# A fused retention and mixture-of-experts kernel: another head, and another order of all instructions

## The chip, the cores and the metric

The kernel runs on one core of a Trainium2 chip. The metric is the time of one execution on the device, in microseconds (us). Engines go by short names: PE is the matrix engine, DVE the vector engine, ACT the scalar engine, POOL is GpSimd and SP the engine that issues most of the transfers. Each engine runs its own instructions in order, and engines wait for each other by semaphores.

## The reference

A linear attention with decay (8 heads of 64, 768 tokens, 4 sequences) gives `x`, and a causal softmax attention of four experts with a gate that picks two of them gives the output. Cut to what matters:

```python
gamma = 1.0 - 2.0 ** (-5.0 - np.arange(H))            # one decay for each head
for t in range(S):
    state = gamma[None, :, None, None] * state + np.einsum('bhd,bhe->bhde', k[:, :, t], v[:, :, t])
    y[:, :, t] = scale * np.einsum('bhd,bhde->bhe', q[:, :, t], state)
x = y.transpose(0, 2, 1, 3).reshape(B, S, H * D)      # 4 x 768 x 512
logits = x @ w_gate                                   # top 2 of 4 experts, softmax over the two
for e in range(E):
    q, k, v = x @ wq[e], x @ wk[e], x @ wv[e]         # 64 columns each
    a = softmax(causal(scale * q @ k.T))
    out += (weight of e for the token) * (a @ v @ wo[e])
```

Everything is fp32. Products that need it are made of three: an operand is split into a high part (`_hi`, `oh`, `xh`) and the rest (`_lo`, `ol`, `xl`), and high times high, high times low and low times high are summed.

## The kernel before, in words

The loop over tokens is done in chunks. Within a chunk, q·k products are masked by `causal` and multiplied into v; what earlier chunks left is a state of 64x64 for each head, multiplied with q; the decays are put in as factors of the position, on k and v before and on the result after. The first sequence begins with three chunks of 128 tokens (`wide`, chunks 0 to 2), because nothing else is there yet to keep PE busy; later chunks have 64 tokens.

`head` (from line 1145) records this beginning. In it stand the loads (`load`, `const`, `wload`); a memset of `wu` on POOL and eight products of `wu` with itself (line 1199), whose results nobody reads; for each wide chunk the q·k products (line 438) into two PSUM tiles, two evictions by DVE that multiply with the mask (line 445), the scaling of v, and from chunk 1 on of k, by the decays in `kd3` (line 426: DVE in chunk 0, POOL in chunks 1 and 2), the masked products with v (line 465), the products of k and v that build the state in PSUM (line 478) and its eviction `sblk` (line 485), and from chunk 1 on the products with the state (line 496). Lines 511 to 515 scale the result by the decays `yb`, which one product with two rows spreads over all partitions (line 1203; ScalarE copies it, line 1205), and split it into `xh` and `xl`. The weights are split in `wsplit` (line 216 on ScalarE, line 217 on DVE or POOL) into `vg_hi` and `vg_lo`, `qk_hi` and `qk_lo`. The gate and value products (line 605, 36 products) follow, then the first projections to q and k (line 563).

After the head, three streams are merged for each following part of a sequence: the chunks of 64 tokens (lines 332, 336, 346 for the state, 391, 397, 405 for the chunk itself), the projections, and the softmax attention (line 739 scores, 790 mask, 809 and 832 to 850 row maxima, 756 exponentials, 875 and 897 sums, 931 products with v, 1033 to 1045 norm and split, 1064 output product). Evictions of the output (lines 1074 and 1078) go into three buffers `ot` and from there to memory (line 1081).

The order is not that of the code. Every operation is recorded by `op` with its engine, what it reads and writes, and a cost; a written table `ORDER` of operation numbers then says in which order all are issued, and `SLOTS` which buffer of its pool each tile takes. Within an engine the order in `ORDER` is the order of execution; a transfer into a buffer waits for the last reader of what stood in it, and with it wait all transfers behind it on SP.

Of the kernel before, what the change touches and what calls it, by code (L numbers as in the profile page):

```python
# [11 lines left out]
AF = mybir.ActivationFunctionType  # L12
# [7 lines left out]
NWARM = 8  # L20
# [89 lines left out]
def tile_retention_moe_attention(  # L110
# [74 lines left out]
    def const(src, shape, name):  # L185
# [5 lines left out]
        op("SP", 0.4, lambda: nc.sync.dma_start(t, src), w=[(name,)], nbytes=n)  # L191
        return t
# [47 lines left out]
    def load(g, which=(0, 1)):  # L240
# [172 lines left out]
    WR = {}  # L413
# [4 lines left out]
    def wide_v(g):  # L418
        nb = LD[g, 1]
        scale = ((1, 0, "v"),) if not g else ((1, 0, "v"), (0, g, "k"))  # L420
        for which, n, tok in scale:
            eng, cost, e = ("DVE", dve_c(512), nc.vector) if not g else ("POOL", pool_c(512), nc.gpsimd)

            def fn(e=e, which=which, n=n):
                x = nb.t[:, which].rearrange("p (h d) -> p h d", d=D)
                e.tensor_tensor(x, x, K["kd3"][:, n, :, None].to_broadcast([128, H, D]), op=OP.mult)  # L426

            op(eng, cost, fn, r=[(nb, tok), ("cst_t",)], w=[(nb, tok)])

    def wide_r1(g):  # L430
# [4 lines left out]
        def fn():  # L435
            for s in range(HP):
                for rt in range(2):
                    nc.tensor.matmul(ps[rt].t[:, s * C:(s + 1) * C], qb.t[rows(rt), 1, s], qb.t[rows(rt), 0, s],
                                     start=True, stop=True)

        op("PE", 512 * 4 * COL + 0.05, fn, r=[(qb, "q"), (qb, "k")], w=[(b,) for b in ps] + [(b, "n") for b in am],
           new=[*ps, *am], mode="64x128")
        for rt in range(2):
            def ev(rt=rt):
                nc.vector.tensor_tensor(am[rt].t.rearrange("p u h t -> p (u h t)").rearrange("p (s t) -> p s t", s=HP),
                                        ps[rt].t.rearrange("p (s t) -> p s t", s=HP),
                                        causal[:, None].to_broadcast([128, HP, C]), op=OP.mult)
# [1016 lines left out]
```

## Time and profile before

The median of 3 runs is 295.76 us (295.52 to 295.77).

| what | before |
|---|---|
| profiled execution | 296.57 us, of which the span is 294.90 |
| PE busy | 286.5 us, 97% of the span |
| DVE busy | 233.3 us, 79% |
| POOL busy | 152.1 us, 52% |
| ScalarE busy | 119.5 us, 41% |
| chain that ended last | PE 89%, DVE 5%, DMA 4% |
| first product, first projection, last product | 1.86, 25.69, 289.94 us |

The profiled execution is one run; the span runs from the first to the last instruction that the profiler saw, and 1.67 us lie around it. An engine's busy time counts overlapped matmuls as pipelined; the chain follows back, from the last instruction, what released each step.

### The profile page before, as it was taken

The page shows a single profiled execution, that of the slowest core. Times are in us where ns is not written, and L with a number is a line of the kernel's source. Part 1 is how long each engine was busy: PE and PEld are TensorE (multiplying, and loading weights), DVE is VectorE, ACT ScalarE, POOL GpSimd, SP SyncE. Part 2 cuts the span into 40 slices and gives each one's busy share as a digit, 9 for nine tenths or more (in the row PEclk, how much of TensorE's full clock was granted, in tenths as well). Part 3 has the DMA queues.
Part 4 walks back from the last instruction along what each step waited for, and adds up shares of the span by engine and source line. Part 5 has one row for each costly group of instructions (what it writes and reads, how often), then busy time and mean ns, then how long its engine had stood idle before and what let it go on. Part 6 is the DMA issues. An engine that isn't in the chain of part 4 may idle for free.

```text
span 294.9 us, 10349 instructions
## 1 busy us (share of the span) xinstructions
PE 286.5 (97%) x4283; PEld 250.8 (85%) x4283; DVE 233.3 (79%) x571; ACT 119.5 (41%) x273; POOL 152.1 (52%) x199
## 2 busy tenths in 40 slices
PE   7899999999999999999999999999999999999993
PEld 3699999988979799898898799998889988977773
DVE  1596478999999688899978468998988888988850
ACT  2151423335433352434542443345533435365462
POOL 2669541343149986235896368305835733089300
PEclk9999999999999999999999999999999999999998
DMA  7995585986874577328915765446204633264023
GB/s 236 408 364 209 181 215 178 250 234 163 253 235 153 153 218 230 101 77 219 320 54 156 247 185 173 96 137 184 57 1 131 179 104 104 53 185 150 15 107 110
DMA packets 22275, 50.33 MB, mean 171 GB/s; under 512 B 4178, under 2 KB 8786, under 8 KB 22228
## 3 DMA queue, kind: packets, MB, share of 16 engines
q1 hardware_dynamic: 22084, 49.60, 55.0%
q8 instruction: 34, 0.56, 0.8%
q14 instruction: 13, 0.11, 0.1%
q10 hardware_dynamic: 144, 0.07, 0.1%
HBM read 30.47 MB, written 6.60 MB: 126 GB/s over the span
## 4 chain that ended last, share of the span: by engine, by line
PE 89%; DVE 5%; DMA 4%; SPq 1%; POOL 1%; issue 0%; ACT 0%; DVEq 0%; POOLq 0%
PE ps L563 22%; PE ps L739 16%; PE ps L931 12%; PE ps L605 12%; PE ps L1064 11%; PE ps L332 5%; PE ps L397 4%; DMA kv_t<-in_kv_dram 2%; PE ps L336 2%; PE ps L391 2%; DMA out_dram<-ot 1%; DVE pm L809 1%; POOL kv_t L426 1%; DVE sz L875 1%; PE ps L496 1%; PE ps L465 1%
## 5 line engine op out<-in xcount | busy, mean ns | idle before, releaser
L809 DVE TRANSPOSE_TENSOR_REDUCE pm<-ps 128x16 f32<-128x512 f32 (+1 forms) x88 | 56.8, 669 | 1.0 <-PE ps L739 0.4
L756 ACT ACTIVATE pt<-ps 128x512 f32<-128x512 f32 (+1 forms) x88 | 46.8, 581 | 24.2 <-PE ps L739 23.9
L739 PE MATMUL ps<-q,k 128*128 128x384 f32 (+5 forms) x320 | 55.3, 309 | 0.3 <-DVE q L850 0.3
L739 PEld LDWEIGHTS ps<-q,k 128*128 128x128 f32 (+1 forms) x320 | 47.8, 189 | 3.7 <-DVE q L850 0.8
L563 PE MATMUL ps<-xh,qk_hi 128*128 128x384 f32 x128 | 43.8, 342 | 0.0
L563 PE MATMUL ps<-xh,qk_lo 128*128 128x384 f32 x128 | 43.1, 336 | 0.0
L563 PE MATMUL ps<-xl,qk_hi 128*128 128x384 f32 x128 | 43.0, 336 | 0.0
L931 PE MATMUL ps<-pt,vt 128*64 128x384 f32 (+2 forms) x320 | 39.7, 394 | 0.0
L897 POOL TENSOR_TENSOR ac<-ac,pt 128x256 f32<-128x256 f32 (+1 forms) x42 | 34.7, 828 | 3.6 <-ACT pt L756 1.5
L568 ACT ACTIVATE k<-ps 128x384 fp32r<-128x384 f32 x32 | 15.7, 492 | 50.6 <-PE ps L563 50.6
L931 PEld LDWEIGHTS ps<-pt,vt 128*64 128x64 f32 x320 | 21.0, 137 | 16.6 <-issue 11.8
L897 POOL TENSOR_TENSOR ac<-pt,pt 128x512 f32<-128x512 f32 x14 | 17.9, 1280 | 24.4 <-ACT pt L756 19.3
L286 POOL TENSOR_TENSOR qd<-qkT_t,qdec_t 128x512 f32<-128x512 f32 (+1 forms) x21 | 25.8, 1232 | 8.9 <-PE ps L336 4.8
L346 DVE TENSOR_TENSOR sblk<-ps,cst_t 128x256 f32<-128x256 f32 x38 | 15.8, 416 | 15.3 <-PE ps L332 11.6
L605 PE MATMUL ps<-vg_hi,xh 128*128 128x260 f32 x96 | 27.7, 289 | 0.0
L605 PE MATMUL ps<-vg_hi,xl 128*128 128x260 f32 x96 | 27.2, 283 | 0.0
L605 PE MATMUL ps<-vg_lo,xh 128*128 128x260 f32 x96 | 27.1, 283 | 0.0
L1010 POOL TENSOR_TENSOR on<-on,fe 128x384 f32<-128x384 f32 x14 | 14.0, 1009 | 25.1 <-ACT pt L756 14.9
L332 PE MATMUL ps<-kv_t 64*64 64x64 f32 x608 | 26.0, 222 | 0.3 <-issue 0.2
L336 PE MATMUL ps<-qd,sblk 64*64 64x64 f32 x624 | 25.9, 221 | 0.0
L271 POOL TENSOR_TENSOR kv_t<-kv_t,cst_t 128x512 f32<-128x512 f32 (+1 forms) x21 | 20.1, 962 | 10.2 <-DMA kv_t<-in_kv_dram 10.2
L790 DVE TENSOR_TENSOR ps<-ps,cneg 128x256 f32<-128x256 f32 (+1 forms) x56 | 20.2, 381 | 6.2 <-PE ps L739 5.9
(128 smaller groups left out, 646.7 us busy)
## 6 DMA issues: line engine op xcount, KB each, us to landing
qkT_t<-in_qkT_dram SPq DMA_DIRECT2D x24, 512.0 KB
kv_t<-in_kv_dram SPq DMA_DIRECT2D x24, 512.0 KB
out_dram<-ot SPq DMA_DIRECT2D x23, 256.0 KB
q<-k SPq DMA_DIRECT2D x28, 192.0 KB
k<-q SPq DMA_DIRECT2D x14, 192.0 KB
k<-k SPq DMA_DIRECT2D x14, 192.0 KB
fe<-fd SPq DMA_DIRECT2D x28, 96.0 KB
pt<-in_wqk_dram SPq DMA_DIRECT2D x4, 256.0 KB
```

Source lines behind the costliest of these rows:

```text
L286: e.tensor_tensor(halves(qd.t), halves(qb.t[:, 0]), K["qdec"][:, :, None, :].to_broadcast([128, HP, n, SC]), op=OP.mult)
L332: nc.tensor.matmul(ST[b].t[rows(rt), s * D:(s + 1) * D], kvs(m, 0, s)[rows(rt)], kvs(m, 1, s)[rows(rt)], start=c == 0 and s == 0, stop=Fal ...
L336: nc.tensor.matmul(yo(m, rt, s), SB[m % 2][rows(rt), s], LD[g, 2].t[rows(rt), s, m % 2 * SC:(m % 2 + 1) * SC], start=m % 2 == 0 and s == 0 ...
L563: nc.tensor.matmul(pb.t[:, :HS], ww[:, kt, wsl], xx[:, kt], start=n == 0, stop=n == 11)
L605: nc.tensor.matmul(pb.t[:, :NV + E], xx[:, kt, sl], ww[:, kt], start=n == 0, stop=n == 11)
L739: nc.tensor.matmul(sb.t[:, col:col + w], k.t[:n, e, ko:ko + C], q.t[:n, e, q0:q0 + w], start=not which and not i, stop=bool(which) and i = ...
L756: op("ACT", act_c(w), lambda: nc.scalar.activation(pt.t[:, :w], sb.t[:, :w], AF.Exp, scale=isc), r=[(sb,)], w=[(pt,)], new=[pt])
L790: lambda: nc.vector.tensor_tensor(at(sb.t), at(sb.t), mask(), op=OP.add),
L809: nc.vector.tensor_reduce(y, src, axis=AX.X, op=OP.max, apply_transpose=True)
L897: op(name, cost, lambda: eng.tensor_tensor(ac.t[:, o:o + w], x.t[:, xo:xo + w], y.t[:, yo:yo + w], op=OP.add), r=[(x,), (y,)], w=[(ac,)], ...
L931: nc.tensor.matmul(ob.t[e * 64:e * 64 + 64, q0:q0 + w], vt.t[:, ko, ee * 64:ee * 64 + 64], PTB[j, p, n].t[:, col:col + w], start=kb == 0, ...
L1064: nc.tensor.matmul(wb.t[:, :n1 - n0], oo[:, sl], ww[:, p, n0:n1], start=n == 0 and p == 0, stop=n == 2 and p == NP - 1)
```

## The change

`const` gets a queue, and `cst` (decays and other columns) is loaded from ScalarE's queue, as its first instruction. The first load of q and k comes in two halves, and the q·k products, the PSUM evictions and their dependences of chunk 0 are cut in the same way. The decay of v is no longer multiplied into v: it is in two masks `DM`, one made by four ScalarE copies of `causal` with a scale for each head, one by a POOL product; all three wide chunks use them, and `kd3` has other factors so that only k is scaled, by POOL, in each of the three. The output decays come as four rows, high parts and rests, which ScalarE copies; one product in one pass spreads them. Eight warm-up products become seven, and two of the same kind (`fill`) stand after the q·k products of chunk 0. `ORDER` and `SLOTS` are new throughout. Line numbers move by a few: 438 is 440 after, 445 is 451, 465 is 469, 478 is 483, 605 is 610, 1033 is 1038, 1064 is 1069, 217 is 218, 346 is 349, 1203 is 1230, 1199 is 1219.

```diff
-NWARM = 8
+NWARM = 7
+NFILL = 2
-            op("SP", 0.4, lambda: nc.sync.dma_start(qb.t, qkT[b, c]), w=[(qb, "hold"), (qb, "q"), (qb, "k")],
-               new=[] if g in HELD else [qb], nbytes=524288)
+            for i, sl in enumerate((slice(0, 2), slice(2, HP)) if not g else (slice(0, HP),)):
+                op("SP", 0.4, lambda sl=sl: nc.sync.dma_start(qb.t[:, :, sl], qkT[b, c][:, :, sl]),
+                   w=[(qb, "half", i)] if not g else [(qb, "hold"), (qb, "q"), (qb, "k")],
+                   new=[] if g in HELD or i else [qb], nbytes=524288 if g else 262144)
...
-        scale = ((1, 0, "v"),) if not g else ((1, 0, "v"), (0, g, "k"))
-        for which, n, tok in scale:
-            eng, cost, e = ("DVE", dve_c(512), nc.vector) if not g else ("POOL", pool_c(512), nc.gpsimd)
...
+        def fn():
+            x = nb.t[:, 0].rearrange("p (h d) -> p h d", d=D)
+            nc.gpsimd.tensor_tensor(x, x, K["kd3"][:, g, :, None].to_broadcast([128, H, D]), op=OP.mult)
...
+        parts = (range(2), range(2, HP)) if not g else (range(HP),)
+        for i, ss in enumerate(parts):
+            def fn(ss=ss):
+                for s in ss:
+                    for rt in range(2):
+                        nc.tensor.matmul(ps[rt].t[:, s * C:(s + 1) * C], qb.t[rows(rt), 1, s], qb.t[rows(rt), 0, s],
+                                         start=True, stop=True)
...
+                    nc.vector.tensor_tensor(x[:, a:a + n], y[:, a:a + n], z[:, a:a + n], op=OP.mult)
...
+        cols = const(cst, [128, 3 * H + 4 * NC * HP + E * E], "cst_t", nc.scalar)
...
+        op("ACT", act_c(640), lambda: nc.scalar.activation(flat(rr.t)[:4, :128 + HP * C], flat(rb.t)[:4, :128 + HP * C],
+                                                           AF.Copy), r=[(rb,)], w=[(rr,)], new=[rr])
...
+        def dm0():
+            for h in range(HP):
+                nc.scalar.activation(DM[0].t[:, h * C:h * C + C], causal, AF.Copy, scale=K["kd3"][:, 0, h:h + 1])
+
+        def dm1():
+            nc.gpsimd.tensor_tensor(DM[1].t.rearrange("p (s t) -> p s t", s=HP),
+                                    causal[:, None].to_broadcast([128, HP, C]),
+                                    K["kd3"][:, 0, HP:, None].to_broadcast([128, HP, C]), op=OP.mult)
...
+        def fill():
+            for i in range(NFILL):
+                nc.tensor.matmul(fb.t, wu, wu[:, None, :].to_broadcast([128, 4, 128]), start=True, stop=True)
...
+        op("PE", 0.24, lambda: nc.tensor.matmul(yp.t, flat(rr.t)[:4, :128], flat(rr.t)[:4, 128:128 + HP * C],
...
-    1, 2, 109, 0, 20, 21, 3, 26, 4, 28, 9, 39, 5, 18, 112, 23, 40, 22, 27, 10, 45, 11, 29, 41, 42, 44, 43, 24,
+    0, 24, 1, 20, 22, 2, 25, 3, 28, 26, 4, 34, 7, 116, 21, 27, 29, 8, 5, 30, 31, 35, 49, 50, 51, 12, 13, 6, 32,
...
-    yrow = np.concatenate([own, yd.reshape(2, H // 2 * C)], axis=1)
+    yd = yd.reshape(2, H // 2 * C).astype(np.float32)
+    top = (yd.view(np.int32) & -4096).view(np.float32)
+    yrow = np.concatenate([np.concatenate([own, own]), np.concatenate([top, yd - top])], axis=1)
```

On SP the fourth load of k and v (chunk 3) goes into buffer `kv_t_2`, which chunk 2 has read, where it went into `kv_t_0`, and it stands behind four loads of q/k weights and masks; behind it come the fifth load of q and k, the last q/k weights, and two more loads of k and v.

Three places of the order are shown. First POOL at the start of the program, before:

```order
L1228 MEMSET k_3_91 32x768
L1146 MEMSET wu 128x128
L1189 MEMSET causal 128x128
L1190 ISA
L1190 AFFINE_SELECT causal<-causal 128x128
```

and after:

```order
L1151 MEMSET wu 128x128
L1196 MEMSET causal 128x128
L1197 ISA
L1197 AFFINE_SELECT causal<-causal 128x128
L1208 TENSOR_TENSOR pt_101<-causal,cst_t 128x512
L426 TENSOR_TENSOR kv_t_66<-kv_t_66,cst_t 128x512
L1255 MEMSET k_4_92 32x768
L426 TENSOR_TENSOR kv_t_67<-kv_t_67,cst_t 128x512
```

The memset of a `k` tile has moved from ahead of `wu` to between the scalings, the mask of line 1208 is new, and each chunk has one scaling.

Second DVE shortly before the first projection, where `qk_lo` is the low part of the q and k weights, `sblk` a state for the chunks of 64 tokens, `am` a masked chunk and `xl` a low part of x. Before:

```order
L405 TENSOR_TENSOR am_71<-ps_147,am_t 128x512
L515 TENSOR_TENSOR xl_75<-ps_146,xh_73 128x4x128
L346 TENSOR_TENSOR sblk_160<-ps_144,cst_t 128x256
L217 TENSOR_TENSOR qk_lo<-pt_101,qk_hi 128x512
L217 TENSOR_TENSOR qk_lo<-pt_104,qk_hi 128x512
L346 TENSOR_TENSOR sblk_159<-ps_144,cst_t 128x256
```

and after:

```order
L520 TENSOR_TENSOR xl_75<-ps_146,xh_73 128x4x128
L218 TENSOR_TENSOR qk_lo<-pt_105,qk_hi 128x512
L349 TENSOR_TENSOR sblk_160<-ps_149,cst_t 128x256
L218 TENSOR_TENSOR qk_lo<-pt_106,qk_hi 128x512
L408 TENSOR_TENSOR am_72<-ps_144,am_t 128x512
```

The state eviction now stands between the two low parts. The products that it waits for (line 332 before, 335 after) stand ahead of the 36 gate and value products on PE before, and behind them after.

Third PE near the end, where `ps_145` before and `ps_146` after take the first chunk of the last output product, and `f` with `ident_t` are the last transposing products of the norm. Before:

```order
L1033 MATMUL ps_146<-f_130,ident_t 64x128 x2
L1033 MATMUL ps_151<-f_130,ident_t 64x128 x2
L1064 MATMUL ps_145<-wo_hi,oh_126 128x512
L1064 MATMUL ps_145<-wo_lo,oh_126 128x512
L1064 MATMUL ps_145<-wo_hi,ol_128 128x512
L1064 MATMUL ps_145<-wo_hi,oh_127 128x512
L1064 MATMUL ps_145<-wo_lo,oh_127 128x512
L1064 MATMUL ps_145<-wo_hi,ol_129 128x512
L1064 MATMUL ps_147<-wo_hi,oh_126 128x512
```

and after:

```order
L1069 MATMUL ps_146<-wo_hi,oh_126 128x512
L1069 MATMUL ps_146<-wo_lo,oh_126 128x512
L1069 MATMUL ps_146<-wo_hi,ol_128 128x512
L1069 MATMUL ps_146<-wo_hi,oh_127 128x512
L1069 MATMUL ps_146<-wo_lo,oh_127 128x512
L1069 MATMUL ps_146<-wo_hi,ol_129 128x512
L1038 MATMUL ps_148<-f_130,ident_t 64x128 x2
L1038 MATMUL ps_150<-f_130,ident_t 64x128 x2
L1069 MATMUL ps_145<-wo_hi,oh_126 128x512
```

The last two groups of transposing products have moved from ahead of the first chunk's six products to behind them.

## Rows read from the trace of the kernel before

**Rows 1.** Page, first part: busy us, share, instructions.

```profile
PE 286.5 (97%) x4283; PEld 250.8 (85%) x4283; DVE 233.3 (79%) x571; ACT 119.5 (41%) x273; POOL 152.1 (52%) x199
```

**Rows 2.** Busy us of each engine by window, then clock and DMA share.

```profile
25.69:290.20 264.51, 263.92 (x3907) 233.03 (x3901) 218.30 (x548) 112.08 (x259) 137.16 (x171) 1.00 0.53 157
```

**Rows 3.** PE's timeline: start, us, line, shapes, count, idle before.

```profile
1.86 3.60 PE L1199 MATMUL ps<-wu 128*128 128x512 bf16 x8 [1.86 <-POOL wu L1146]
5.38 1.67 PE L438 MATMUL ps<-qkT_t 64*128 64x128 f32 x16
...
8.51 1.09 PE L465 MATMUL ps<-am,kv_t 128*64 128x128 f32 x16 [0.85 <-DVE am L445]
9.54 1.16 PE L438 MATMUL ps<-qkT_t 64*128 64x128 f32 x16
10.63 1.12 PE L1203 MATMUL ps<-vt 2*128 2x512 f32 x2
12.21 0.69 PE L478 MATMUL ps<-kv_t 128*64 128x64 f32 x16 [0.47 <-POOL kv_t L426]
...
16.33 1.04 PE L465 MATMUL ps<-am,kv_t 128*64 128x128 f32 x16
```

**Rows 4.** The same timeline of POOL.

```profile
0.81 0.73 POOL L1228 MEMSET k<- 32x768 f32 x1 [0.29 <-POOLq L1452]
1.60 0.20 POOL L1146 MEMSET wu<- 128x128 bf16 x1
...
10.12 2.04 POOL L426 TENSOR_TENSOR kv_t<-kv_t,cst_t 128x512 f32<-128x512 f32 x2 [2.14 <-DMA kv_t<-in_kv_dram]
...
21.66 2.98 POOL L217 TENSOR_TENSOR qk_lo<-pt,qk_hi 128x512 fp32r<-128x512 f32 x2 [1.93 <-ACT qk_hi L216]
```

**Rows 5.** The same timeline of DVE.

```profile
6.19 0.69 DVE L426 TENSOR_TENSOR kv_t<-kv_t,cst_t 128x512 f32<-128x512 f32 x1 [6.19 <-DMA cst_t<-in_cst_dram]
7.17 1.29 DVE L445 TENSOR_TENSOR am<-ps,causal 128x512 f32<-128x512 f32 x2 [0.29 <-PE ps L438]
8.38 0.42 DVE L485 TENSOR_TENSOR sblk<-ps,cst_t 128x256 f32<-128x256 f32 x1
...
21.94 3.25 DVE L217 TENSOR_TENSOR qk_lo<-pt,qk_hi 128x512 fp32r<-128x512 f32 x2
```

**Rows 6.** DMA rates of 0 to 10 us in 40 slices.

```profile
GB/s 0 0 0 0 0 0 0 164 115 229 311 360 377 344 393 393 426 459 353 274 194 127 241 360 320 357 311 360 311 328 377 393 442 377 426 442 426 410 393 410
```

**Rows 7.** Timeline of ScalarE in the tail: a copy of 128x128.

```profile
284.80 0.26 ACT L1038 ACTIVATE on<-ps 128x128 f32<-128x128 f32 x1
```

**Rows 8.** Longest pieces of the chain, first 30 us: start, us, what.

```profile
3.45 6.54 DMA kv_t<-in_kv_dram
...
19.62 4.58 PE ps L605 x36
```

**Rows 9.** Busy times by window, around PE's idle time in the body.

```profile
50.00:55.00 5.00, 5.00 (x128) 4.93 (x119) 4.96 (x11) 1.73 (x4) 2.28 (x2) 1.00 0.87 235
55.00:60.00 5.00, 4.87 (x119) 4.54 (x117) 4.71 (x13) 1.08 (x4) 1.32 (x2) 1.00 0.98 229
60.00:65.00 5.00, 4.83 (x61) 3.96 (x61) 4.56 (x14) 2.86 (x6) 3.40 (x7) 1.00 0.73 219
```

**Rows 10.** The chain from 285 us on.

```profile
285.15 0.44 PE ps L1033 x8
...
287.26 0.61 ACT ot L1078
...
287.89 3.86 DMA out_dram<-ot
```

**Rows 11.** Timelines of PE, DVE and ScalarE: the last instruction of each.

```profile
289.94 0.27 PE L1064 MATMUL ps<-wo_hi,ol 128*128 128x128 f32 x1
...
291.87 0.29 DVE L1074 COPY ot<-ps 128x128 f32<-128x128 f32 x1 [4.17 <-DMA out_dram<-ot]
...
292.19 0.37 ACTq L1081 DMA_DIRECT2D out_dram<-ot  x1
```

More of the change, by code (lines that the diff above doesn't have):

```diff
@@ L183, in tile_retention_moe_attention, with const @@
     consts = {}
-    def const(src, shape, name):
+    def const(src, shape, name, queue=nc.sync):
         t = sbuf.tile(shape, F32, name=name)
@@ L190, in const @@
             n *= x
-        op("SP", 0.4, lambda: nc.sync.dma_start(t, src), w=[(name,)], nbytes=n)
+        op("SP", 0.4, lambda: queue.dma_start(t, src), w=[(name,)], nbytes=n)
         return t
@@ L419, in wide_v @@
         nb = LD[g, 1]
-        scale = ((1, 0, "v"),) if not g else ((1, 0, "v"), (0, g, "k"))
-        for which, n, tok in scale:
-            eng, cost, e = ("DVE", dve_c(512), nc.vector) if not g else ("POOL", pool_c(512), nc.gpsimd)
[L424 to L428, printed above, removed]
+        def fn():
+            x = nb.t[:, 0].rearrange("p (h d) -> p h d", d=D)
+            nc.gpsimd.tensor_tensor(x, x, K["kd3"][:, g, :, None].to_broadcast([128, H, D]), op=OP.mult)
+        op("POOL", pool_c(512), fn, r=[(nb, "k"), ("cst_t",)], w=[(nb, "k")])
     def wide_r1(g):
@@ L433, in wide_r1, with ev @@
         WR[g] = am
[L435 to L447, printed above, removed]
-            op("DVE", dve_c(512), ev, r=[(ps[rt],), ("causal",)], w=[(am[rt],)])
+        parts = (range(2), range(2, HP)) if not g else (range(HP),)
[5 more added lines that the diff above has]
+                                         start=True, stop=True)
+            op("PE", 128 * len(ss) * 4 * COL + 0.05, fn, r=[(qb, "q"), (qb, "k")] if g else [(qb, "half", i)],
+               w=[(b, i) for b in ps] + [(b, i, "n") for b in am], new=[] if i else [*ps, *am], mode="64x128")
+        for i, ss in enumerate(parts):
+            for rt in range(2):
+                def ev(rt=rt, a=ss[0], n=len(ss)):
+                    x = am[rt].t.rearrange("p u h t -> p (u h t)").rearrange("p (s t) -> p s t", s=HP)
+                    y = ps[rt].t.rearrange("p (s t) -> p s t", s=HP)
+                    z = DM[rt].t.rearrange("p (s t) -> p s t", s=HP)
+                    nc.vector.tensor_tensor(x[:, a:a + n], y[:, a:a + n], z[:, a:a + n], op=OP.mult)
+                op("DVE", dve_c(128 * len(ss)), ev, r=[(ps[rt], i), (DM[rt],)], w=[(am[rt], i)])
     def wide_dg(g):
@@ L466, in fn @@
                                      start=s == 0, stop=not g and s == HP - 1, skip_group_check=True)
-        op("PE", 512 * 4 * COL + 0.02, fn, r=[(LD[g, 1], "v"), (am[0],), (am[1],)], w=ww, new=new, mode="128x64")
+        op("PE", 512 * 4 * COL + 0.02, fn, r=[(LD[g, 1], "v")] + [(a, i) for a in am for i in range(1 if g else 2)], w=ww, new=new,
+           mode="128x64")
     def wide_st(g):
@@ L1193, in head @@
         op("POOL", 0.6, mkcausal, w=[("causal",)])
+        DM[:] = [Buf(PT), Buf(PT)]
+        def dm0():
[5 more added lines that the diff above has]
+                                    K["kd3"][:, 0, HP:, None].to_broadcast([128, HP, C]), op=OP.mult)
+        op("ACT", 1.15, dm0, r=[("causal",), ("cst_t",)], w=[(DM[0],)], new=[DM[0]])
+        op("POOL", pool_c(512), dm1, r=[("causal",), ("cst_t",)], w=[(DM[1],)], new=[DM[1]])
         op("POOL", 0.4, mkwn, w=[("wn0",)])
@@ L1338 @@
     "gs": "0000",
[L1339 to L1341 removed]
+    "k1": "0123420314023012",
+    "k2": "0123402132410341",
+    "kv_t": "012012202101202102101121",
     "lg": "0101",
@@ L1429, in _layouts @@
     kd3[:, 0] = by_tile(gam)[None] ** (-s[:, None, None].astype(np.float64))
-    kd3[:, 1] = by_tile(gam)[None] ** -float(C)
-    kd3[:, 2] = by_tile(gam)[None] ** -float(2 * C)
+    for g in (1, 2):
+        kd3[:, g] = kd3[:, 0] * by_tile(gam)[None] ** -float(g * C)
     kd3 = kd3.reshape(C, 3, H)
```

37 lines of the change are left out of this document (17 added, 20 removed), and 156 rows, old and new, of the table ORDER.

## The prediction

> **What bounds the kernel now.** I read the page's first part, then the busy times by stage, then the timelines of the first 26 us engine by engine, the longest pieces of the chain of waits there, and last the chain and timelines of the final 10 us. The reader should see a TensorE-bound program: PE is busy 97% of the span [rows 1], and in the 264.51 us from the first projection at 25.69 us to the last product it lacks only 0.59 us (264.51 less 263.92 [rows 2]). So there are three places to win: the head up to 25.69 us, those 0.59 us, and the tail, in which PE has nothing left to do.
>
> In the head PE starts at 1.86 us because it waits for the `wu` memset, which stands on POOL behind a 0.73 us memset [rows 3, 4]. The first q·k products run at 5.38 us with no wait shown, so the first load has landed by then. Chunk 0's masked products wait 0.85 us for DVE's two mask evictions (1.29 us together), and chunk 1's `kv` products start at 12.21 us, just behind POOL's pair of scalings [rows 3 to 5]. In the chain a 6.54 us load of `kv` stands ahead of that pair [rows 8]. In the tail the first chunk of the last output product is evicted at 287.26 us, its transfer takes 3.86 us, and DVE's copy of the last chunk, whose product is done at about 290.2 us, waits for that transfer because both use buffer `ot_2`; its own transfer is issued at 292.19 us and the span ends at 294.90 us [rows 10, 11].
>
> **The start.** `wu` is now POOL's first memset, so it moves from 1.60 to about 0.81 us and PE from 1.86 to about 1.07 us. Seven products at 3.60/8 us each [rows 3, 4] take 3.15 us: PE is free at about 4.2 us, not 5.4.
>
> **First load in halves.** Bytes flow from about 1.75 us [rows 6]; each figure there is for 0.25 us. Summed, 262 KB have come by 2.9 us and 524 KB by 3.6 us; with 68 KB of `cst` now sharing the engines from ScalarE's queue, 3.1 and 3.8. What a semaphore adds is not shown; the other end is 5.38 us [rows 3]. I take the nearer half of that span for the first half, 4.2 us, and 5.0 for the second. Sixteen products took 1.67 us [rows 3], so each half costs 0.84: 4.2 to 5.05, then 5.05 to 5.9, against an end of 7.05 before.
>
> **Masks and evictions.** The scaling of v by DVE (0.69 us) goes, but it hid behind the products: DVE waited 0.29 us after it [rows 5], so by itself it is worth nothing. Four evictions of 128x256 replace two of 128x512; the same shape costs 0.42 us [rows 5]. The first pair is done at 5.9, the second at about 6.8 to 7.0: chunk 0's masked products start at about 7.0, not 8.51. This needs both masks by 5.1 us. POOL's takes about 1.02 (half of the pair's 2.04 [rows 4]), ScalarE's four copies of 128x128 about 4 x 0.26 [rows 7], both after `cst`, which lands between 3.1 and 5 us: up to 0.9 us late in the worst case, 0 as taken. The two filler products (at most 2 x 0.45) stand in PE's gap from 5.9 to 7.0 and cost nothing while that gap holds.
>
> **Rest of the head.** The products of `kv` for chunk 0 (0.69) no longer fill the gap but follow it; the spread of output decays goes from two passes, 1.12 us, to one, at least 0.56 [rows 3]. Its ScalarE copy of 4x640 is not in the trace; between 0.26 (128x128 [rows 7]) and 0.76 (0.61 for 512 columns, scaled by 640/512 [rows 10]), it lies beside the evictions. POOL scales only k of chunks 1 and 2, 1.02 us less for each, so the wait ahead of 12.21 goes. Next is DVE: chunk 1's q·k products run at about 8.05 to 9.2, two evictions (1.29) end at 10.6, and that, not POOL, releases chunk 1's masked products, while PE fills 1.25 of the 1.4 us. From there masked products (1.04), q·k products (1.16), `kv` products (0.69), products with the state (not in these rows; as many as the masked ones, so 1.04) and `kv` products again (0.69) put chunk 2's masked products at about 15.2 (15.0 to 15.5) against 16.33 [rows 3]. By PE's work alone the first projection would start 1.05 us earlier, at 24.65.
>
> **What is late next.** The projection needs the last low part `qk_lo`. Before, DVE did two of them back to back from 21.94 to 25.19 us, 0.5 us ahead of need. Now the second stands behind the state eviction `sblk_1`, which waits for the state products of the 64-token chunk that PE does only after the gate/value products (4.58 us [rows 8]). Those began at 19.62 and would end at about 22.7 us. The chunk's products (half of the 1.5 us that two small chunks filled from 24.2 to 25.69) and the 0.42 us eviction end at 23.9, and then `qk_lo` takes 0.68 us alone (as the 1.29 for two masks) or 1.63, the mean of the two (3.25 together) that ran beside POOL's [rows 4, 5]: 24.6 to 25.55. POOL again scales in that stretch, so I take 25.3, i.e. 0.4 us gained in the head, between 1.05 gained and 0.35 lost (25.55 and half of the masks' 0.9 on top). The Trainium skill, SBUF — State Buffer, section "SBUF: two separate sides", says that the port pair of DVE and GpSimd is an exclusive lock held for a whole instruction when DVE reads two SBUF inputs. By it a loser would pay a whole POOL instruction (1.02 of a scaling to 1.49, half of the pair's 2.98 [rows 4]) on top of 0.68, up to 2.2, and the projection would start at 25.7 or later; the trace's mean of 1.63 agrees with the low end, so the rule speaks against this place of `qk_lo`.
>
> Also behind a wait: the fourth `kv` load goes into the buffer that chunk 2's masked products read last, so SP holds back the next q/k load, a weight load and two more `kv` loads until about 16 us. Issued there and landing within about 4 us, it is early enough for the state products at 22.7 us; at the 6.54 us of the longest piece [rows 8] plus POOL's 1.05 it is not, and costs up to 0.8 us at the projection.
>
> **The body.** Same products, other order. At most 0.59 us is to be won [rows 2]; half of it (0.13 and 0.17) lies at 55 to 65 us, where DVE is busy 4.71 and 4.56 us of 5, after 4.96 in the 5 us before [rows 9], and PE starts on late state products. There the new order puts about 1.0 us more DVE work ahead of that eviction (gate operations and one row maximum more, one sum less) and about 0.9 us more PE work ahead of the product that needs it. I take 0.2 us gained, between 0.59 gained and 1.5 lost.
>
> **The tail.** The first chunk's products now stand ahead of two transposing groups that came before it, so its eviction comes 0.44 us (those two groups of four, 8 products in 0.44 us [rows 10]) earlier relative to the last product, and the chain of eviction (0.61), transfer, copy (0.29) and issue moves with it [rows 10, 11]. The transfer may take 3.86 again, or less: if 2.3, the copy is released by its product at 290.2 instead, 1.6 us sooner than now. I take 0.45 gained, between 1.0 gained and 0.3 lost.
>
> **The sum.** 0.4 + 0.2 + 0.45 = 1.05 us. The profiled execution took 296.57 us (294.90 in the span, 1.67 around it), 0.81 above the median 295.76, so 295.52 for it and 294.7 for the median.
>
> **Rivals.** A: the head's gain is lost at `qk_lo` (lock or late `kv` load): the projection starts at 25.7 as before; body gains nothing, the tail 0.25: 295.5. For it: one DVE queue, two slow rows; against: PE's earlier start pulls everything ahead. B: PE's work is the only limit in the head (1.05), and the tail's transfer is quick (0.9): 293.8. For it: `qk_lo` at 0.68 ends before 24.65; against: all of POOL's scalings have to fall elsewhere. C, slower: the state eviction in the stretch at 55 to 65 us. DVE is full there, so if the extra PE work does not in fact lie ahead of the late product, 1.0 us more of DVE is 1.0 us of PE wait; with DVE operations lengthened by POOL as `qk_lo` was, twice more by 0.5: 2.0 lost, 0.85 won elsewhere: 296.9. It decides from 1.45 us of extra wait on. For it: DVE is at 4.96 and 4.71 of 5 us ahead of it; against: PE lacked only 0.30 us there. D: the tail's order does nothing, as the transfer that ends last is late for a reason of its own, and the head gives 0.4, the body 0.2: 295.15.
>
> **Chances.** Within 0.2% means 295.17 to 296.35, about what a measurement can tell from no change. My forecast has 0.40 (own range 294.1 to 295.2), A 0.24, B 0.15, C 0.16, D 0.05. Faster: the forecast nearly whole, B and part of D, 0.57; same: A, the rest of those and C's mild end, 0.28; slower: 0.15. The range takes in A and most of B and stops short of C's worst: 293.6 to 296.5.
>
> **What would show it.** PE's first product near 1.07 us; chunk 0's masked products near 7.0; chunk 2's near 15.2; the first projection at 25.3 with a wait for DVE's `qk_lo` ahead of it (24.65 and none would be B; 25.7 or later A); PE lacking under 0.6 us from there to its last product (over 2 would be C); the last copy's wait under 4.17 us by about 0.4. I am wrong if the head's gain is not there at the first projection, or if a wait that no row of before shows opens in the body.

## The result and the profile after

The changed kernel was forecast at 294.7 us. Its median was 299.6 us (297.69 to 300.53, 6 runs) beside 295.82 us for the kernel before: a ratio of 1.0107, 95% interval [1.0070, 1.0144], slower. Its times differ more from session to session than those of the kernel before: the same file, timed twice more on other chips, gave 1.0028 [0.9999, 1.0058] and 1.0051 [1.0026, 1.0077], with medians of 297.08 and 297.50 us, where those of the kernel before lie between 295.57 and 295.84 in all sessions. In none of the three was it faster; the two later ones put the price at 0.3%, which is not clear of none, and at 0.5%, and the first session saw the bad end of it. Ratios, and the profiles that are read below, leave out the runs in which the chip was disturbed.

The profiled execution took 299.6 us, with a span of 297.9 us, 3.0 more than before. What lies around the span was 1.67 to 1.81 us in every run of the kernel before, and 1.68 to 1.74 in this first session of the changed one; in some runs below it is more, and no view shows what it holds. The page of the changed kernel, busy time and share of the span by engine:

```profile
PE 291.1 (98%) x4283; PEld 253.5 (85%) x4283; DVE 234.1 (79%) x572; ACT 122.3 (41%) x278; POOL 151.2 (51%) x199
```

Against [rows 1], PE is busy 4.6 us more for the same number of instructions, so products became longer by the profile's count. Of the 4.6 us, 3.1 lie ahead of the first projection, 0.6 in the middle and 0.9 in the last stage, as the windows show; first of the kernel before, then after: from the first projection to the first selecting product (line 954, 959 after) of the last stage, from there to the last product, and the rest. Columns as in [rows 2].

```profile
25.69:280.03 254.34, 253.75 (x3807) 225.22 (x3801) 213.93 (x533) 106.17 (x241) 137.16 (x171) 1.00 0.54 159
280.03:290.22 10.19, 10.19 (x101) 7.82 (x100) 4.37 (x15) 5.91 (x18) 0.00 (x0) 1.00 0.29 108
290.22:294.90 4.68, 0.00 (x0) 0.00 (x0) 0.29 (x1) 0.00 (x0) 0.00 (x0) 0.82 0.30 107
```

```profile
27.86:283.24 255.38, 254.34 (x3808) 225.70 (x3802) 214.38 (x532) 107.52 (x242) 137.76 (x175) 1.00 0.55 161
283.24:294.30 11.06, 11.06 (x101) 7.79 (x100) 5.43 (x18) 5.08 (x16) 0.00 (x0) 1.00 0.27 101
294.30:297.90 3.60, 0.00 (x0) 0.00 (x0) 0.29 (x1) 0.00 (x0) 0.00 (x0) 0.82 0.39 135
```

So the head lost 2.17 us (27.86 against 25.69), the long middle 1.04, the last stage 0.87, and what follows the last product gained 1.08: 3.0 in all. The head is the largest, and its timeline of PE, which answers to [rows 3], shows two things at once:

```profile
1.06 3.17 PE L1219 MATMUL ps<-wu 128*128 128x512 bf16 x7 [1.06 <-POOL wu L1151]
4.25 1.23 PE L440 MATMUL ps<-qkT_t 64*128 64x128 f32 x8
5.69 1.61 PE L440 MATMUL ps<-qkT_t 64*128 64x128 f32 x8 [0.21 <-DMA qkT_t<-in_qkT_dram]
7.23 1.04 PE L1227 MATMUL ps<-wu 128*128 128x512 bf16 x2
9.09 1.98 PE L469 MATMUL ps<-am,kv_t 128*64 128x128 f32 x16 [0.82 <-DMA kv_t<-in_kv_dram]
11.00 2.08 PE L440 MATMUL ps<-qkT_t 64*128 64x128 f32 x16
...
15.47 1.16 PE L440 MATMUL ps<-qkT_t 64*128 64x128 f32 x16
```

The first is the wait: chunk 0's masked products start at 9.09 us, not for DVE as before but for the load of `kv`. The chain of the first 14 us has it as one piece:

```profile
2.18 6.78 DMA kv_t<-in_kv_dram
```

Before, SP issued that load at 1.25 us and nobody waited for it. Here SP needs 1.32 us for the two halves ahead of it:

```profile
0.80 1.32 SPq L254 DMA_DIRECT2D qkT_t<-in_qkT_dram  x2
2.18 0.59 SPq L262 DMA_DIRECT2D kv_t<-in_kv_dram  x1
```

The second is the length of the products. Sixteen masked products take 1.98 us against 1.09 in [rows 3], the next sixteen q·k products 2.08 against 1.16; by 15.47 us they are at 1.16 again. I read that as TensorE at the lower of its two levels, 1.2 instead of 2.4 GHz: before, the products had become short during the first q·k products (1.67 us for sixteen, the next sixteen 1.16), after an unbroken row of work since 1.86 us; here PE paused at 5.48 and again at 8.27 us, and they became short only some 14 us into the span. The granted clock of the window view reads 1.00 throughout, so this is read from durations alone, and no row names the level. The Trainium skill, TensorE: Matmul & The Clock Gate, Part 1, says that the array's clock depends on how busy PE has been recently; the durations of this profile agree with that, and a second profile of the same file, below, shows that the pauses alone do not decide it.

### The profile page after: what moved, and what is told of

Its sections match the earlier page's. It is cut to its first block, busy times and chain, and to the rows that moved or that the text cites. A ratio compares the mean times of both kernels' runs of the same rounds, so it can differ in the third digit from the quotient of the medians.

```text
span 297.9 us, 10351 instructions
## 1 busy us (share of the span) xinstructions
PE 291.1 (98%) x4283; PEld 253.5 (85%) x4283; DVE 234.1 (79%) x572; ACT 122.3 (41%) x278; POOL 151.2 (51%) x199
## 4 chain that ended last, share of the span: by engine, by line
PE 91%; DMA 3%; issue 1%; SPq 1%; POOL 1%; ACT 1%; DVE 0%; POOLq 0%; ACTq 0%
PE ps L568 21%; PE ps L744 16%; PE ps L610 12%; PE ps L936 12%; PE ps L1069 11%; PE ps L335 5%; PE ps L400 4%; DMA kv_t<-in_kv_dram 2%; PE ps L394 2%; PE ps L339 2%; PE ps L469 1%; DMA fe<-fd 1%; SPq L254 1%; PE ps L440 1%; POOL on L1015 1%
## 5 line engine op out<-in xcount | busy, mean ns | idle before, releaser
L814 DVE TRANSPOSE_TENSOR_REDUCE pm<-ps 128x16 f32<-128x512 f32 (+1 forms) x88 | 57.4, 675 | 3.6 <-PE ps L744 2.2
L744 PE MATMUL ps<-q,k 128*128 128x384 f32 (+5 forms) x320 | 56.3, 311 | 0.0
L289 POOL TENSOR_TENSOR qd<-qkT_t,qdec_t 128x512 f32<-128x512 f32 (+1 forms) x21 | 25.3, 1208 | 6.3 <-PE ps L339 3.1
L335 PEld LDWEIGHTS ps<-kv_t 64*64 64x64 f32 x608 | 21.3, 134 | 4.8 <-issue 2.9
```

The costliest lines, as they stand in the source:

```text
L289: e.tensor_tensor(halves(qd.t), halves(qb.t[:, 0]), K["qdec"][:, :, None, :].to_broadcast([128, HP, n, SC]), op=OP.mult)
L335: nc.tensor.matmul(ST[b].t[rows(rt), s * D:(s + 1) * D], kvs(m, 0, s)[rows(rt)], kvs(m, 1, s)[rows(rt)], start=c == 0 and s == 0, stop=Fal ...
L744: nc.tensor.matmul(sb.t[:, col:col + w], k.t[:n, e, ko:ko + C], q.t[:n, e, q0:q0 + w], start=not which and not i, stop=bool(which) and i = ...
L814: nc.vector.tensor_reduce(y, src, axis=AX.X, op=OP.max, apply_transpose=True)
```

## The experiments

Three theories: the pauses that hold the clock down (1), the halves of the first load, with runs of 1 KB, that make `kv` late (2), and the new order of the body (3).

**More warm-up products.**

```diff
-NWARM = 7
+NWARM = 11
```

> The changed kernel with 11 warm-up products instead of 7, so that TensorE works without a gap from 1.06 us until past the landing of both halves. Theory 1 (the head lost because TensorE paused at 5.48 and again at 8.27 us and so stayed at its lower clock until about 14.4 us): the masked products of chunk 0 still start near 9.0 us, where their load lands, but take about 1.05 us instead of 1.98, the next q.k products 1.16 instead of 2.08; the first projection starts near 26.0 instead of 27.93, the whole about 1.8 us shorter than the changed kernel. Theory 2 (the late load of kv alone is the cause, the clock is not tied to the pauses): durations stay at 1.98 and 2.08, and the time is that of the changed kernel within 0.3 us. Theory 3 (the order of the body is the cause): the head may move, but the end is still over 1.5 us later than the kernel before.

Measured: 1.0060 [1.0035, 1.0086]. The timeline of PE of this run:

```profile
1.06 4.88 PE L1219 MATMUL ps<-wu 128*128 128x512 bf16 x11 [1.06 <-POOL wu L1151]
5.87 1.04 PE L440 MATMUL ps<-qkT_t 64*128 64x128 f32 x10
7.29 0.71 PE L440 MATMUL ps<-qkT_t 64*128 64x128 f32 x6 [0.39 <-DVE am L451]
8.46 1.23 PE L469 MATMUL ps<-am,kv_t 128*64 128x128 f32 x16
9.62 1.16 PE L440 MATMUL ps<-qkT_t 64*128 64x128 f32 x16
```

All are short, in spite of a pause of 0.39 us: the clock had risen before it. The first projection stands at 26.69 us, 1.2 us earlier than in the profile above; theory 1 had put it near 26.0. What holds it there is no longer PE: it waits 0.4 us for ScalarE's `qk_hi`, which itself waited 4.7 us for the load of its weights. The whole, at 1.0060, is shorter than in the first session of the changed kernel, but not shorter than in its two later ones, so no gain in time is shown.

**Halves as runs of 2 KB.** The layout of chunk 0 is permuted, so that a half is contiguous; the second half of the products' operands is addressed to match.

```diff
+    qkT[0, 0] = qkT[0, 0].reshape(128, 2, 2, 2, C).transpose(0, 2, 1, 3, 4).reshape(128, 2, H // 2, C)
...
-                op("SP", 0.4, lambda sl=sl: nc.sync.dma_start(qb.t[:, :, sl], qkT[b, c][:, :, sl]),
+                op("SP", 0.4, lambda i=i: nc.sync.dma_start(half(qb, i), half0(qkT, b, c, i)) if not g else
```

> The changed kernel with the first load of q and k laid out so that each half is one run of 2 KB for each partition instead of two runs of 1 KB. Theory 2 (runs of 1 KB take the transfer engines nearly as long as 2 KB, so the load of kv behind them lands at 8.96 us instead of about 6): kv lands near 7 us, the wait of 0.82 us ahead of the masked products goes, and with it, as the pauses of TensorE shrink, up to 2 us. Theory 1 (the clock alone): the second pause shrinks only if the load comes earlier; if kv still lands near 9 us nothing moves.

Measured: 1.0004 [0.9967, 1.0041]; no difference from the kernel before, within an interval that is 0.7% wide. The same file stands again in the table at the end of this section.

**Fewer warm-up products in the kernel before.**

```diff
-NWARM = 8
+NWARM = 4
```

> The kernel before with 4 warm-up products instead of 8, nothing else: TensorE ends them at about 3.65 us and pauses until its first load lands, by 5.38 us at the latest. Theory 1: the lower clock lasts past the next pause, the masked products of chunk 0 take up to 2.0 us instead of 1.09 and the q.k products of chunk 1 up to 2.1 instead of 1.16, and the kernel is 1 to 2 us slower. Rival: the clock rises a set time after the first product whatever lies between, or the POOL scalings at 12.2 us hide it: no change within 0.3 us.

Measured: 1.0001 [0.9962, 1.0040]. Its timeline of PE:

```profile
4.50 2.08 PE L438 MATMUL ps<-qkT_t 64*128 64x128 f32 x16 [0.76 <-DMA qkT_t<-in_qkT_dram]
6.75 1.12 PE L478 MATMUL ps<-kv_t 128*64 128x64 f32 x16 [0.17 <-DVE kv_t L426]
8.04 1.98 PE L465 MATMUL ps<-am,kv_t 128*64 128x128 f32 x16 [0.17 <-DVE am L445]
9.95 1.16 PE L438 MATMUL ps<-qkT_t 64*128 64x128 f32 x16
12.09 0.69 PE L478 MATMUL ps<-kv_t 128*64 128x64 f32 x16
```

The products are long, as theory 1 has it (2.08 and 1.98 us), but no cost is shown: at 12.09 us the `kv` products of chunk 1 start where they did before, at 12.21. There PE had waited 0.85 us for DVE and 0.47 us for POOL [rows 3]; here longer products fill that time, and the first of them start at 4.50 us instead of 5.38. Theory 1 holds for the clock in this profile and fails for the price in this kernel: slow products matter only where nothing else is late. In the changed head POOL has half the scalings, so that cover is smaller; this was argued, not tried.

**The new order on the old head.** The tables `ORDER` and `SLOTS` of the changed kernel, mapped to the operations of the kernel before. In this run one scaling stands behind its reader: the masked products of chunk 1 use v before its decay.

```diff
-    1, 2, 109, 0, 20, 21, 3, 26, 4, 28, 9, 39, 5, 18, 112, 23, 40, 22, 27, 10, 45, 11, 29, 41, 42, 44, 43, 24,
+    0, 1, 20, 2, 18, 3, 26, 21, 23, 5, 110, 22, 6, 4, 27, 41, 42, 43, 10, 11,
```

> The kernel before, its head in the old form (one load, two mask evictions, scalings of v, spread in two passes, eight warm-up products, no fillers), with the order table and the buffer slots of the changed kernel, mapped instruction by instruction. Theory 3 (the order of the body costs about 1.9 us from the first projection to the last product, the tail gives 1.1 back): first projection near 25.7, the stretch to the last product near 266.4 instead of 264.3 us, whole about 0.8 us slower than the kernel before. If the head alone is the cause: as fast as before or up to 1.1 us faster, by the tail.

Measured: 1.0131 [1.0072, 1.0190], with the first projection at 30.12 us: the order is not made for this head (PE waits 2.6 us for POOL's scalings and 2.3 us for DVE's mask evictions). The rest can be read all the same, in the windows as above:

```profile
30.12:284.38 254.26, 254.15 (x3802) 225.07 (x3802) 214.84 (x532) 107.42 (x242) 137.91 (x175) 1.00 0.54 161
284.38:295.43 11.05, 11.05 (x101) 7.79 (x100) 5.42 (x18) 5.08 (x16) 0.00 (x0) 1.00 0.26 99
295.43:298.86 3.43, 0.00 (x0) 0.00 (x0) 0.29 (x1) 0.00 (x0) 0.00 (x0) 0.93 0.40 142
```

The middle is as long as before (254.26 against 254.34); the last stage has the changed kernel's 11.05 us, to 0.01. The head adds a row on the clock: the sixteen q·k products at 4.58 us take 1.27 us, and after the 2.3 us wait the masked products take 1.94 us again.

**The old order on the new head.** From chunk 1 on the tables of the kernel before.

```diff
-    0, 24, 1, 20, 22, 2, 25, 3, 28, 26, 4, 34, 7, 116, 21, 27, 29, 8, 5, 30, 31, 35, 49, 50, 51, 12, 13, 6, 32,
+    0, 24, 1, 20, 22, 2, 25, 3, 28, 26, 115, 4, 34, 5, 21, 27, 29, 30, 31, 6, 35, 11, 47, 7, 118, 48, 12, 52, 13,
```

> The changed kernel's head (halves with 1 KB runs, masks with the decay, one-pass spread, seven warm-up products, fillers) with the order and the buffer slots of the kernel before from chunk 1 on. If the order is the cause of the longer body: the stretch from the first projection to the last product falls from 266.4 us to about 264.3 (as in the kernel before), TensorE busy in it about 264.0 instead of 265.4. If the body is longer for another reason (the data layout, the new constants): it stays near 266. The head stays slow by the clock, first projection between 26 and 28 us; whole 0 to 2 us slower than the kernel before.

Measured: 1.0037 [1.0021, 1.0053]; first projection at 25.57 us, then

```profile
25.57:280.09 254.52, 253.89 (x3809) 225.21 (x3802) 214.00 (x533) 106.05 (x241) 137.44 (x171) 1.00 0.54 159
280.09:290.27 10.18, 10.18 (x101) 7.81 (x100) 4.38 (x15) 5.91 (x18) 0.00 (x0) 1.00 0.29 108
290.27:294.30 4.03, 0.00 (x1) 0.00 (x0) 0.29 (x1) 0.00 (x0) 0.00 (x0) 0.76 0.34 123
```

The stretch is 264.70 us, as expected; the last stage is 10.18 again. So 0.87 us of the longer body belong to the new order, whatever the head is: the last stage takes 10.18 or 10.19 us in five profiles with the old order and 11.00 to 11.07 in nine with the new. In this run the clock rose early although the halves were of 1 KB and PE paused 0.16 us: the changed head does not always lose it.

**Both causes removed.** Runs of 2 KB and `NWARM = 9`.

> The changed kernel with halves as one 2 KB run for each partition and 9 warm-up products: TensorE has neither of its two pauses before the masked products of chunk 0 by more than some tenths. If the two causes of the late head are the clock and the 1 KB runs: masked products of chunk 0 at about 7.7 us and at 1.05 us, first projection at or below 25.7, but bounded by the last q/k weights (their load waits on SP) near 26; whole within 0.5 us of the kernel before. If only one counts, as in the runs with one of the two: first projection near 26.7.

Measured: 1.0002 [0.9983, 1.0021]; first projection at 25.13 us, 0.56 before the old one. PE waits 0.5 us ahead of it for `qk_hi`, as in the run with 11 products. The last weight load is issued behind the `kv` load that SP holds back, and lands seven microseconds later:

```profile
17.35 0.42 SPq L211 DMA_DIRECT2D pt<-in_wqk_dram  x1
24.45 0.63 ACT L217 ACTIVATE qk_hi<-pt 128x512 fp32r<-128x512 f32 x1 [4.26 <-DMA pt<-in_wqk_dram]
25.11 0.69 DVE L218 TENSOR_TENSOR qk_lo<-pt,qk_hi 128x512 fp32r<-128x512 f32 x1 [1.45 <-ACT qk_hi L217]
25.13 0.44 PE L578 MATMUL ps<-xh,qk_hi 128*128 128x384 f32 x1 [0.55 <-ACT qk_hi L217]
```

**The same head with the old order, and two variants of it:** the last 41 operations in the new order; POOL's scaling of chunk 1 (operation 52) moved ahead of three memsets and a split (118, 48).

```diff
-    35, 11, 47, 7, 118, 48, 12, 52, 13, 49, 50, 51, 32, 36, 37, 33, 38, 14, 63, 55,
+    35, 11, 47, 7, 12, 52, 13, 49, 50, 51, 32, 36, 37, 33, 38, 14, 63, 55, 56, 39,
```

> Head of the changed kernel with 2 KB runs and 9 warm-up products, order and slots of the kernel before from chunk 1 on. If head and order add: first projection at 24.7 to 25.3 us, stretch to the last product 264.3, tail 4.6: about 0.5 to 1 us faster than the kernel before. If the load of the weights or POOL sets the first projection whatever the head does: 25.7, no change.

Measured: 1.0007 [0.9992, 1.0023]. The first projection stood at 25.05 us in this profile, but at 25.56 and 25.78 in those of the two variants, with the same first part of the head: in them the first ten q·k products took 1.60 and 1.65 us instead of 0.93. Half a microsecond of head is not there in every execution. On the same chip the old order on the head of 1 KB and seven products had 1.0037 (296.59 us against 295.83): both causes together cost 0.8 us by the medians there, with intervals that just touch.

> As the run before it, and the last 41 operations in the order of the changed kernel, in which the first chunk of the last output product stands ahead of the last two transposing groups. If that order is what shortened the end from the last product on from 4.6 to 3.6 us: again 3.5 to 3.7 us, the last copy on DVE right behind its product, 0.5 to 1 us faster than the run before it. If the late transfer there was chance: no difference beyond 0.3 us.

Measured: 1.0055 [1.0039, 1.0071], 0.5% slower than without. Last stage 11.18 us instead of 10.18, the end after it 3.98 instead of 3.79. A new wait of PE has come in:

```profile
PE ps L1048 <- ACT on L1053: 0.4, 1, 0.4
```

> Head of the changed kernel with 2 KB runs and 9 warm-up products, order of the kernel before from chunk 1 on, and POOL's scaling of chunk 1 ahead of three memsets and a weight split. If POOL's place is what TensorE waits 0.71 us for ahead of chunk 1's kv products: that wait shrinks below 0.35, first projection at 24.6 to 24.8 instead of 25.05, whole 0.3 to 0.9 us faster than the kernel before. If the load of chunk 1 sets it: no change from the run without it.

Measured: 1.0013 [0.9991, 1.0035]; the wait ahead of chunk 1's `kv` products is still 0.71 us, a miss. Nor is it the load of chunk 1, the expectation's other reading: POOL's scaling behind that load is done a microsecond earlier.

```profile
10.00 1.04 POOL L433 TENSOR_TENSOR kv_t<-kv_t,cst_t 128x512 f32<-128x512 f32 x1 [2.00 <-DMA kv_t<-in_kv_dram]
11.58 0.41 DVE L500 TENSOR_TENSOR sblk<-ps,cst_t 128x256 f32<-128x256 f32 x1
12.10 0.69 PE L493 MATMUL ps<-kv_t 128*64 128x64 f32 x16 [0.71 <-issue]
```

The products start 0.11 us after DVE has read chunk 0's state out of the PSUM tile to which they add; the same 0.11 us lie between the two in the three other runs that have a new head and the old order. The profile names no releaser here, so by the rows DVE's eviction is the likely one; no run tried it.

**The changed kernel again.** No edit.

> The changed kernel once more, unaltered, beside the others of this call on one chip. If the late load and the low clock of its first profile belong to the kernel: first 4 us of transfers from 2 to 6 us again near 255 GB/s, the kv load of chunk 0 waited for, first projection after 26.5 us, ratio 1.007 to 1.014. If that profile was an unlucky one: first projection near 25.5 and a ratio near 1.003, as for the same head with the old order.

Measured: 1.0028 [0.9999, 1.0058]; 12 times from 295.52 to 301.37 us. In this profile the clock was up in time:

```profile
4.16 1.23 PE L440 MATMUL ps<-qkT_t 64*128 64x128 f32 x8
5.98 0.71 PE L440 MATMUL ps<-qkT_t 64*128 64x128 f32 x8 [0.60 <-DMA qkT_t<-in_qkT_dram]
6.63 0.61 PE L1227 MATMUL ps<-wu 128*128 128x512 bf16 x2
8.08 1.09 PE L469 MATMUL ps<-am,kv_t 128*64 128x128 f32 x16 [0.84 <-DMA kv_t<-in_kv_dram]
9.24 1.16 PE L440 MATMUL ps<-qkT_t 64*128 64x128 f32 x16
```

First projection at 25.64 us, level with before: even so the head's gain is gone, in the waits for the second half and for `kv` (1.44 us together). The two expectations were mixed up in one: the late load is the kernel's own, the low clock comes and goes. And it is not the pauses alone that decide: they are longer here than in the first profile (0.60 and 0.84 us against 0.21 and 0.82). The middle was 254.36 us, the last stage 11.07. This execution's span, 294.6 us, is 0.3 shorter than that of the kernel before; its time, 297.07 us, is longer because 2.47 us lie around the span.

**2 KB runs with a pause.** `NWARM = 4`.

> The changed kernel with 2 KB runs and only 4 warm-up products: TensorE pauses from 2.9 us until its first half lands at about 4 us, nothing else differs from the run with 2 KB runs and seven. Clock theory: the products run at the slow length (1.98 us for the 16 masked ones) past chunk 0, in part past chunk 1's q.k products, first projection 0.5 to 1.5 us later than with 9 warm-up products (25.1) and the kernel 0.2 to 0.5% slower than with 9. Rival (pauses do not matter, the waits for loads and evictions cover the slow products): no difference beyond 0.3 us.

Measured: 1.0051 [1.0026, 1.0076], 0.5% above the run with 9 products, whose time came from another chip. PE paused 1.16 us before its first half:

```profile
4.11 1.65 PE L450 MATMUL ps<-qkT_t 64*128 64x128 f32 x10 [1.16 <-DMA qkT_t<-in_qkT_dram]
5.95 1.22 PE L450 MATMUL ps<-qkT_t 64*128 64x128 f32 x6 [0.19 <-DVE am L461]
7.09 1.04 PE L1237 MATMUL ps<-wu 128*128 128x512 bf16 x2
8.06 1.97 PE L479 MATMUL ps<-am,kv_t 128*64 128x128 f32 x16
9.96 1.47 PE L450 MATMUL ps<-qkT_t 64*128 64x128 f32 x16
```

Long products without a late `kv`: the clock by itself, first projection at 26.44 us. Not all of the 0.5% is the clock, though: the median span is 0.85 us longer than with 9 products, and in 9 of the 12 executions 2.28 to 2.98 us lie around the span, against 1.67 to 1.87 with 9. Why is open.

Over all profiles that are read here, the masked products of chunk 0 are long (1.97 or 1.98 us) in both with 4 warm-up products, in one of four with 7, and in none of nine with 8 to 11; a tenth, the old head in the new order, has 8 and is long behind a wait of 2.3 us.

**The old end in the new order.** 2 KB, 9 products, the last 73 operations as before.

> The changed kernel with 2 KB runs and 9 warm-up products, its last 73 operations in the order of the kernel before. If the order of the end costs TensorE 0.86 us (11.05 us from the first selecting product to the last product in every run with the new end, 10.19 in every run with the old): 10.2 us again, last product 0.85 us earlier; the time after it 3.6 to 4.6. Whole 0.3 to 0.9 us faster than the run with the new end. If the 0.86 us come from what stands ahead of the last 73 operations: 11 us again, no change.

Measured: 1.0031 [1.0006, 1.0055], against 1.0002 with the new end, on another chip. Windows:

```profile
279.77:290.29 10.52, 10.52 (x101) 7.95 (x100) 4.97 (x17) 5.91 (x18) 0.00 (x0) 1.00 0.27 100
290.29:294.70 4.41, 0.00 (x1) 0.00 (x0) 0.29 (x1) 0.00 (x0) 0.00 (x0) 1.00 0.34 123
```

PE gives back 0.53 of the 0.86 us, and the end takes it: 4.41 us instead of 3.61. Around the span lie 2.05 to 2.13 us in every execution, 0.3 more than with the new end. The gain expected did not come. The rest of the 0.86 us stands ahead of the last 73 operations, or in how the two orders meet; that is open.

**The two-by-two table, on one chip.**

> First of four on one chip: runs of 1 KB or 2 KB in the halves of the first load, 7 or 9 warm-up products. This is the changed kernel itself. If both the late kv load and the late rise of the clock cost: the slowest of the four, ratio 1.003 to 1.010, with the widest spread of its times.

> 2 KB runs, 7 warm-up products. If the load alone is the cause: as fast as the run with 2 KB and 9, ratio 1.000. If the clock alone: as slow as the run with 1 KB and 7.

> 1 KB runs, 9 warm-up products, TensorE busy until about 5 us. If the clock alone is the cause: as fast as the run with 2 KB and 9. If the load alone: as slow as the run with 1 KB and 7; masked products of chunk 0 wait for kv until 8 us or later either way.

> 2 KB runs, 9 warm-up products. If both count: the fastest of the four, first projection near 25.1 us, narrowest spread, ratio 0.998 to 1.002; what is left against the kernel before is then the order of the end (0.86 us more of TensorE) against the head's half us.

| | 7 warm-up products | 9 |
|---|---|---|
| runs of 1 KB | 297.50 us, 1.0051 [1.0026, 1.0077] | 296.97 us, 1.0024 [0.9998, 1.0051] |
| runs of 2 KB | 296.52 us, 1.0020 [0.9996, 1.0044] | 295.88 us, 1.0002 [0.9982, 1.0023] |

By the medians the runs cost 1.0 us, the warm-up 0.6, and they add. Neighbours in the table overlap in their intervals, so the size of each by itself is not settled; the corners do not overlap, so that both together cost about half a per cent is. The first projections of the profiles part the two more clearly, in us, for the new order:

| | masked products of chunk 0 in 1.09 to 1.23 us | in 1.97 or 1.98 us |
|---|---|---|
| runs of 1 KB | 25.64, 26.51, 26.69 | 27.86 |
| runs of 2 KB | 24.69, 25.13, 25.18, 25.33 | 26.44 |

The 1 KB run with 9 products shows the load alone, its products at full clock:

```profile
9.43 1.09 PE L469 MATMUL ps<-am,kv_t 128*64 128x128 f32 x16 [1.35 <-DMA kv_t<-in_kv_dram]
```

and the 2 KB run with 9 products has no wait for `kv`:

```profile
8.01 1.23 PE L479 MATMUL ps<-am,kv_t 128*64 128x128 f32 x16
```

Why `kv` is late is in the transfers from 2 to 6 us: packets, bytes, rate, packets by size. First of the run with 1 KB and 9 products, then with 2 KB and 9:

```profile
DMA packets 725, 0.85 MB, mean 212 GB/s; under 512 B 51, under 2 KB 659, under 8 KB 725
```

```profile
DMA packets 592, 1.22 MB, mean 305 GB/s; under 512 B 62, under 2 KB 190, under 8 KB 592
```

The kernel before moved 310 GB/s in that stretch, the changed one 255 in its first profile and 226 in its second; over all profiles it is 212 to 255 in five with runs of 1 KB and 296 to 345 in the eleven others. SP has a part in it: it issued `kv` at 1.71 us with runs of 2 KB, at 2.18 with runs of 1 KB. How much of the lateness is the later issue and how much the slower transfers, the runs do not separate. The Trainium skill, DMA: Bandwidth & Descriptors, Specifications, gives 512 B as the least transfer for full rate; here packets of 1 KB at the head of the queue went with a rate lower by a fifth to a third, and the measurement decides.

## Why the prediction was wrong

*The start* was right: PE at 1.06 us (1.07 forecast), seven products until 4.23 (4.2).

*The first half* came at 4.16 to 4.25 us (4.2). The second came at 5.69 and 5.98 instead of 5.0, and a half of the products took 1.23 us, not 0.84: I halved 1.67 us, in which the clock had risen under way, although [rows 3] show 1.16 for sixteen products of the same shape further down. That pair of rows was the sign that the head runs on a clock that is not yet up, and the prediction has no term for it.

*Chunk 0's masked products near 7.0 us* is the step that failed: they started at 9.09, and at 8.08 with the clock up. I named the masks and the evictions as their conditions and never gave the load of `kv` a landing time, because no row of before shows anybody waiting for it. Cutting the load ahead of it in runs of 1 KB made it late: it was issued 0.93 us later than before (2.18 against 1.25) and held PE 0.82 and 0.84 us. With 2 KB and 9 products nobody waits for it, and they started at 7.41 and 8.01 us in two profiles. Chunk 2's masked products, forecast at 15.2 us, stood at 18.71 and 16.03, and at 15.36 with 2 KB and 9.

*The masks* were to be there by 5.1 us. ScalarE's were done at 5.41, because a table load of 1.28 us, which the sum does not have, stands between `cst` and its copies. Here that cost nothing, as the first half's products ended at 5.48. With runs of 2 KB `cst` itself lands 1.4 to 1.7 us later (ScalarE goes on at 4.20 to 4.47 us instead of 2.74 to 2.83), and with 7 products the first eviction waits for POOL's mask: what the better runs give `kv`, they take in part from `cst`.

*What is late next* was right in the place and wrong in the kind. Where the head is quick, the first projection waits for the last weights, but for `qk_hi`, ahead of `qk_lo`, and because of a load: the prediction names that weight load among those held back by SP, but gives a landing time and a price (up to 0.8 us) only to the `kv` load ahead of it. With 2 KB and 9 products it went out at 17.35 us and released ScalarE at 24.45. DVE then does the last `qk_lo` in 0.69 us, not 1.63, since POOL is not beside it, so the exclusive port had no case there; the one before it took 1.38 us in the first profile, beside POOL's scaling. With both causes removed the first projection stands at 25.13 and 25.33 us: the forecast of 25.3 holds for that kernel, not for this one. The run with the old end has the same head, and there it stands at 24.69, near rival B's 24.65.

*The body* was to gain 0.2. Rival C was wrong as well: no state eviction opened a wait at 55 to 65 us. The middle took 254.36 us in one profile, 255.38 in the other, and over all profiles it is no longer with the new order than with the old (253.97 to 255.38 against 254.15 to 255.16); in the slower one a single wait, 0.7 us at 84 us ahead of line 394, stands out, and its cause is open. The 0.87 us in the last stage I had not looked for; the 24 selecting products take 1.35 us instead of 0.86 there: DVE's last sums, which they read, end at 284.12 us while they run, where before they ended at 279.71, ahead of them. The rest lies in transposing (2.04 against 1.82 us) and output products (5.07 against 4.77).

*The tail* gained 1.08 where 0.45 was forecast, but part of it was never there: before took 4.68 us in its profile, and 3.90 in the variant with 4 warm-up products, whose end is the same code. Rival D said that the late transfer had a reason of its own, and that is nearer; moving the products ahead was paid on PE. Last stage and end together take 14.52 to 14.80 us in nine profiles with the new order, and 13.96 to 14.21 in four with the old beside the 14.87 of the profile on which the forecast was built: the new end loses about half a microsecond where 0.45 was to be gained.

So of the 3.0 us, by the first profile, 2.2 are the head (late `kv` and low clock), 0.9 the last stage, 1.0 a middle that is not always longer and whose cause is open, less 1.1 at the end, of which 0.8 was the luck of one profile.

## What to carry to other kernels

When a load is cut or moved, write down a landing time for every load behind it, also for those that nobody waited for before. Where two rows of the same products differ in length in the first microseconds, the clock is still down there: in these runs fewer products ahead of the first load went with long products more often, for up to ten microseconds, and whether this costs depends on what else is late. A gain at the end of a program should be taken from more than one profile, and a gain in the span checked against the time around it.

## What was not expected of the hardware

With the second half of the load in time, PE still paused 0.18 to 0.58 us after its tenth q·k product, put down to DVE's eviction: the second half's products write the PSUM tiles that DVE is reading the first half from. In seven profiles PE goes on 0.05 or 0.06 us after the end of DVE's first eviction, which speaks for it; a kernel with other tiles was not tried. And one and the same head had its first ten products in 0.93 us in one profile and in 1.65 in another: the moment at which the clock rises is not fixed by the program alone.
